# The last multiply-add of a convolution goes from VectorE to ScalarE and GpSimd, and the order of all engines is laid out anew

## The chip, the cores and the metric

One core of a Trainium2 chip runs the whole kernel. The metric is the device time of one execution in microseconds (us), the median of three runs. TensorE (PE) multiplies, VectorE (DVE), ScalarE (ACT) and GpSimd (POOL) do the elementwise work, SyncE (SP) issues the DMAs.

## The reference

```python
scores = q @ k.T / sqrt(64)                       # 8 batches x 8 heads, 576 x 576, q and k 576 x 64
thresh = max(scores, -1) - tau
attn = where(scores >= thresh, exp(scores - max(scores, -1)), 0)
attn = attn / (sum(attn, -1) + 1e-9)
x = concat_heads(attn @ v)                        # 8 x 576 x 512
pre = sum(conv_w[i] * xp[:, i:i+576, :] for i in range(5))   # causal, xp has 4 zero rows in front
out = (sigmoid(pre) * (x @ w_val)) @ w_out        # the weights arrive as float64
```

## The kernel before

**Units of work.** The 64 heads are worked off in 32 pairs (8 batches of 4 pairs). A pair has nine score tiles of 128 rows by 576 keys: one that holds the 64 left-over rows of both heads, and eight of 128 queries of one head; 288 tiles in all. For each tile PE makes the scores `s` in PSUM from split operands (`KH`, `KL`, `Q`; `multiply`, L732, four matmuls), DVE takes the negative row maximum `nm` (`largest`, L736) and the row threshold `th` from it, one number a row (`lowest`, L742), ACT makes `e = exp(s - max)` (`weigh`, L746), and DVE keeps what lies above the threshold, with the row sum (`keep`, L753, into `pp`, `sums`). `keep` sets the score room in PSUM free. There are two such rooms, and a third one until tile `THIRD_UNTIL`, which then becomes the two accumulators `acc` of the products.

**Behind the tiles.** The row sums get their 1e-9 on POOL (L770) and are inverted on DVE (L772); the division of `pp` goes to POOL (L783), ACT (L779) or DVE (L781), whichever is first. PE turns `pp` by matmuls with an identity (`turn`, L836, into `tp`), ACT copies it to `T` (L847), and PE multiplies by `v` (L914, L922). ACT puts the result of a pair into `xT` (L932).

**The convolution** (`convolve`) is done per pair on 128 channels by 576 rows: the first of the five multiply-adds makes `pre` on POOL (`tap0`, L988), the other four run on DVE (`tap`, L993, one instruction each of the form `pre = xT * cw + pre`), and ACT makes the tanh of the gate (L1001). ACT and POOL split `xT` into `xh` and `xl` (L969, L975).

**The products** (`products`, L1052) run once a batch: 96 matmuls for `x @ w_val`, gated by DVE (`val`, L1079), split into `gh` and `gl` (L1100 on ACT, L1107 on POOL), and 96 for the product with `w_out`, taken out by DVE (L1142) or ACT (L1144). The float64 weights are turned into float32 parts by integer steps on DVE, ACT and POOL during the first batch (L321 to L385).

**What sets the order.** The program is laid out by a planner that runs when the kernel is built. Each step is an `op` with an engine, a due time and a planned cost. The due time is the number of the tile plus an offset from a table, `EARLY` for the first 78 tiles and `AT` behind it. `carry_out` takes again and again the step that can begin first, by lowest due time among those, and writes it on its engine. In the plan a DVE step between SBUF operands (`DVEp`) and a POOL step never run at the same time. On the chip each engine then works its list off in that order, and waits by semaphores. Where the plan leaves PE idle in the first part, `keep_busy` (L181) puts in matmuls of the identity whose result nobody reads, one per so many planned us of gap:

```python
if e == "PE" and 1.0 < gap and t < FILL_UNTIL and r_tp.free and r_tp.free[0][0] <= idle["PE"] + 0.2:
    keep_busy(r_tp.free[0][1], int(gap / 0.5))
```

Of the kernel before, what the change touches and what calls it, by code (L numbers as in the profile page):

```python
# [19 lines left out]
DIVIDE = ("DVEp", "ACT")  # L20
PACE_M = 0.124
THIRD_UNTIL = 38
LOWEST = 0
SHARED = (0, 1, 3, 6, 7)
REST = 'DVE'
SPREAD = False
ALONE = 0
AMONG = ("DVEp",)
# [10 lines left out]
AT = dict(
    score=-33.05, largest=-102.51, lowest=-23.11, weigh=-37.49, keep=-24.88, add=23.1, inv=-56.23,  # L40
    divide=59.56, turn=-22.26, copy=19.76, attend=-23.83, evac=-22.31, fetch=96.26, high_k=128.92,
    low_k=67.78, scale_q=4.66, high_q=12.66, low_q=1.99, place=-132.6, copies=-77.08, copies_q=56.7,
    fetch_v=22.69, prep=-27.65, early1=49.11, early2=54.51, early3=29.03, conv_high=20.77,
    tap0=-0.84, conv_low=-16.76, tap=-34.66, tap_step=11.87, gate=-12.05, products=-6.3, val=94.33,
    g_high=43.79, g_low=162.74, out=99.25, send=53.84, words=-4.76, words_step=7.01,
    words_fetch=0.77, split=35.72, words_sub=-25.09, words2=-1.91, cw=-6.65, corner=-6.73,
)

EARLY = dict(
    score=-5.33, largest=-82.82, lowest=163.7, weigh=-36.29, keep=13.11, add=-6.03, inv=-37.4,  # L50
    divide=28.57, turn=0.66, copy=-20.26, attend=2.02, evac=-61.15, fetch=97.48, high_k=23.73,
    low_k=18.92, scale_q=50.26, high_q=46.36, low_q=8.75, place=15.59, copies=54.04,
    copies_q=165.86, fetch_v=25.8, prep=-4.29, early1=15.1, early2=13.7, early3=23.08,
    conv_high=21.07, tap0=-30.63, conv_low=22.96, tap=5.74, tap_step=0.34, gate=-109.04,
    products=14.86, val=-11.89, g_high=20.21, g_low=13.29, out=-36.55, send=-68.92, words=-5.8,
    words_step=8.17, words_fetch=-14.64, split=119.57, words_sub=9.29, words2=-3.84, cw=-128.53,
    corner=-82.08,
)
# [6 lines left out]
def tile_thresholded_attention_gated_mix(  # L65
# [64 lines left out]
    def due_of(k, what, at=None):  # L130
        return k + (EARLY if (k if at is None else at) < EARLY_UNTIL else AT)[what]
# [62 lines left out]
    def carry_out():  # L194
        while True:
# [764 lines left out]
    def convolve(pair, batch, k, js):  # L960
# [29 lines left out]
        def tap(i):  # L990
# [283 lines left out]
```

## Time and profile before

| | |
|---|---|
| median of 3 runs (lowest to highest) | 731.37 us (730.84 to 732.71) |
| the profiled execution: its time, and its span from first to last instruction | 730.5 us, 728.7 us |
| busy share of the span | PE 96%, PE's weight loads (PEld) 84%, DVE 91%, ACT 81%, POOL 64% |
| DMA, share of 16 engines | 53% |

Busy time counts a stretch in which at least one instruction of the engine is under way. Instructions of one engine overlap at their ends, so the sum of their durations is more than the busy time. The time of the execution is 1.8 us more than its span.

### The profile page before, as it was taken

Reading aid. Unit: us, or ns where it says so; the run is one execution under the profiler, and the core shown is the slowest. Engines: PE = TensorE matmul, PEld = TensorE weight load, DVE = VectorE, ACT = ScalarE, POOL = GpSimd, SP = SyncE. Lnnn points to the kernel's source line nnn. Section 1 sums busy time; section 2 is a strip of 40 time slices with the busy share of each in tenths; the row PEclk is TensorE's granted clock in tenths of the full one; section 3 lists DMA queues with packets and bytes.
Section 4 is the critical chain, followed back from the end, with each engine's and each line's share of the span. In section 5 each row is a group of like instructions: output and inputs, shape, how many; then the busy total and the mean of one; then the engine's idle time right before and its main releaser. Section 6 shows DMA issues by size and latency. Waiting matters only on the chain.

```text
span 728.7 us, 16203 instructions
## 1 busy us (share of the span) xinstructions
PE 702.0 (96%) x5272; PEld 609.2 (84%) x5272; DVE 660.2 (91%) x1618; ACT 591.6 (81%) x1167; POOL 467.8 (64%) x690
## 2 busy tenths in 40 slices
PE   7789888999999999999999999999999999999998
PEld 6566656888888998888889898888988888898988
DVE  7999998999999988999999999999999999899842
ACT  6999997898878898877889887887878887898730
POOL 3788677887677747686566765677456865655231
PEclk9999999999999999999999999999999999999999
DMA  6886655537565666356664655556664446540001
GB/s 219 211 203 181 164 137 156 113 87 184 165 147 126 151 178 152 98 137 159 158 152 113 152 149 152 129 125 168 160 160 117 112 137 169 144 98 19 34 33 66
DMA packets 60883, 100.54 MB, mean 138 GB/s; under 512 B 18688, under 2 KB 20096, under 8 KB 60800
## 3 DMA queue, kind: packets, MB, share of 16 engines
q1 hardware_dynamic: 60512, 98.96, 53.1%
q8 instruction: 42, 0.69, 0.4%
q10 hardware_dynamic: 288, 0.56, 0.2%
q14 instruction: 41, 0.34, 0.1%
HBM read 35.18 MB, written 9.44 MB: 61 GB/s over the span
## 4 chain that ended last, share of the span: by engine, by line
PE 83%; DVE 7%; ACT 5%; DMA 2%; issue 1%; POOL 1%; SPq 0%; ACTq 0%; POOLq 0%; DVEq 0%
PE acc L1052 26%; PE s L732 19%; PE tp L836 17%; PE acc L922 9%; PE tp L922 6%; DVE pp L753 2%; PE acc L914 2%; DVE nm L736 2%; ACT e L746 2%; PE tp L914 2%; ACT T L847 1%; ACT pp L779 1%; DMA pre<-w_out 1%; DVE pre L993 1%; PE tp L181 1%
## 5 line engine op out<-in xcount | busy, mean ns | idle before, releaser
L736 DVE TENSOR_REDUCE nm<-s 128x1 f32<-128x576 f32 x276 | 204.8, 753 | 22.0 <-PE s L732 18.2
L746 ACT ACTIVATE e<-s,nm 128x576 f32<-128x576 f32 x276 | 204.2, 753 | 13.9 <-DVE nm L736 11.8
L753 DVE SCALAR_TENSOR_TENSOR pp<-s,th,e 128x576 f32<-128x576 f32 x244 | 196.8, 812 | 9.6 <-ACT e L746 5.6
L847 ACT COPY T<-tp 128x384 f32<-128x384 f32 x384 | 175.0, 493 | 18.3 <-PE tp L836 17.0
L836 PE MATMUL tp<-ident,pp 128*128 128x128 f32 x1152 | 176.9, 274 | 8.6 <-ACT T L847 4.6
L732 PE MATMUL s<-KH,Q 128*128 128x288 f32 x488 | 147.7, 320 | 8.4 <-DVE pp L753 3.5
L836 PEld LDWEIGHTS tp<-ident,pp 128*128 128x128 f32 x1152 | 137.2, 140 | 16.9 <-ACT T L847 6.8
L732 PE MATMUL s<-KL,Q 128*128 128x288 f32 x488 | 135.9, 295 | 0.0
L783 POOL TENSOR_SCALAR pp<-pp,sums 128x576 f32<-128x576 f32 x132 | 105.9, 807 | 25.6 <-DVE sums L772 10.7
L993 DVE SCALAR_TENSOR_TENSOR pre<-xT,cw,pre 128x576 f32<-128x576 f32 x128 | 120.5, 943 | 0.7
L732 PEld LDWEIGHTS s<-KH,Q 128*128 128x128 f32 x488 | 92.0, 188 | 23.1 <-issue 9.8
L779 ACT ACTIVATE pp<-pp,sums 128x576 f32<-128x576 f32 x102 | 79.3, 790 | 23.1 <-DVE sums L772 22.6
L770 POOL TENSOR_SCALAR sums<-sums 128x2 f32<-128x2 f32 (+1 forms) x160 | 44.6, 279 | 76.6 <-DVE pp L753 63.3
L732 PEld LDWEIGHTS s<-KL,Q 128*128 128x128 f32 x488 | 92.1, 189 | 0.0
L1052 PE MATMUL acc<-xh,wvh 128*128 128x256 f32 (+1 forms) x256 | 78.5, 307 | 1.6 <-ACT xT L891 1.3
L1052 PE MATMUL acc<-gh,woh 128*128 128x256 f32 (+1 forms) x256 | 78.8, 308 | 0.0
L1052 PE MATMUL acc<-gh,wol 128*128 128x256 f32 (+1 forms) x256 | 78.5, 307 | 0.0
L1052 PE MATMUL acc<-xh,wvl 128*128 128x256 f32 (+1 forms) x256 | 78.4, 306 | 0.0
L1052 PE MATMUL acc<-gl,woh 128*128 128x256 f32 (+1 forms) x256 | 78.1, 305 | 0.0
L1052 PE MATMUL acc<-xl,wvh 128*128 128x256 f32 (+1 forms) x256 | 77.8, 304 | 0.0
L461 POOL TENSOR_TENSOR ql<-q_r,qh 128x320 fp32r<-128x320 f32 (+1 forms) x62 | 59.1, 969 | 23.3 <-ACT qh L455 20.0
L447 POOL TENSOR_TENSOR kl<-k_r,kh 128x320 fp32r<-128x320 f32 x62 | 57.2, 929 | 22.7 <-ACT kh L441 12.9
(116 smaller groups left out, 1386.9 us busy)
## 6 DMA issues: line engine op xcount, KB each, us to landing
KH<-kh SPq DMA_DIRECT2D x124, 144.0 KB, 2.6
KL<-kl SPq DMA_DIRECT2D x124, 144.0 KB, 3.2
v<-vs SPq DMA_DIRECT2D x32, 320.0 KB, 3.1
k_r<-kT SPq DMA_DIRECT2D x31, 320.0 KB, 3.9
q_r<-qT SPq DMA_DIRECT2D x31, 288.0 KB, 3.2
outT<-o SPq DMA_DIRECT2D x28, 288.0 KB, 2.1
Q<-qh SPq DMA_DIRECT2D x62, 128.0 KB, 2.7
Q<-ql SPq DMA_DIRECT2D x62, 128.0 KB, 3.6
```

Of the source, the lines that this page charges most:

```text
L461: engine.tensor_sub(self.ql[:, x:y], self.q_r[:, x:y], self.qh[:, x:y].bitcast(F32))
L732: nc.tensor.matmul(s[:, a, :HS], w, m, start=i == 0, stop=i == len(terms) - 1)
L736: nc.vector.tensor_reduce(self.nm, self.s[:, :, :HS], axis=AX.XY, op=ALU.max, negate=True)
L746: nc.scalar.activation(self.e, self.s[:, :, :HS], AF.Exp, bias=self.nm)
L753: nc.vector.scalar_tensor_tensor(grp.p[:, i * S : (i + 1) * S].rearrange("p (a f) -> p a f", a=2), self.s[:, :, :HS], self.th, self.e, op0 ...
L779: nc.scalar.mul(v, v, ri(i))
L783: nc.gpsimd.tensor_scalar(v, v, ri(i), 0.0, op0=ALU.mult, op1=ALU.add)
L836: nc.tensor.transpose(tp[:, i * P : (i + 1) * P], self.p[:, k0 : k0 + P], ident)
L847: engine(T[:, c0 : c0 + n, self.off : self.off + P], tp[:, 0 : n * P].rearrange("p (c q) -> p c q", q=P),)
L922: nc.tensor.matmul(a[hs, : W[half.j]], t.v[:, c0 : c0 + D], half.T[:, h * NKC + c, 0 : W[half.j]], start=False, stop=c == NKC - 1, skip_gr ...
L993: nc.vector.scalar_tensor_tensor(cv, pair.xT[:, i + a : i + z], cw[:, g, i : i + 1], cv, op0=ALU.mult, op1=ALU.add)
L1052: nc.tensor.matmul(taken[name, e, j][:, :w], wt[:, c, c0 : c0 + P], moving(c, i)[:, hs], start=n == 0, stop=n == NM - 1,)
```

## The change

- The last of the four multiply-adds on DVE (`i = 4`) becomes two steps: ACT multiplies `xT` by the weight into a new room `tmp` (L1007 of the changed kernel), and POOL adds `tmp` to `pre` (L1013). There is one `tmp`; `ql` has one room instead of two.
- The row threshold (L742) may go to POOL for any tile (`LOWEST` 0 to 300), where the planner finds POOL free earlier.
- The unread matmuls in PE's gaps are counted by `(gap - 0.6) / 0.115` instead of `gap / 0.5`.
- All due offsets are others, the third score room stays until tile 42 instead of 38, the products are spaced by 0.421 instead of 0.124 of a tile, and two planned costs are larger (one DMA issue 0.62 instead of 0.58, a POOL step with two inputs by 0.04).

```diff
-PACE_M = 0.124
-THIRD_UNTIL = 38
-LOWEST = 0
+PACE_M = 0.421
+THIRD_UNTIL = 42
+LOWEST = 300
...
+APART = (4,)
...
-    score=-33.05, largest=-102.51, lowest=-23.11, weigh=-37.49, keep=-24.88, add=23.1, inv=-56.23,
+    score=-80.76, largest=-174.57, lowest=-22.68, weigh=-66.2, keep=-108.45, add=93.41, inv=-170.32,
...
-                keep_busy(r_tp.free[0][1], int(gap / 0.5))
+                keep_busy(r_tp.free[0][1], int((gap - 0.6) / 0.115))
...
+        def scaled(i):
+            def run():
+                room["tmp"] = r_tmp.take()
+                nc.scalar.mul(room["tmp"], pair.xT[:, i + a : i + z], cw[:, g, i : i + 1])
+
+            return run
+
+        def added():
+            cv = batch.pre[:, g, a:z]
+            nc.gpsimd.tensor_add(cv, cv, room["tmp"])
...
         for i in range(1, KT):
-            last = op("DVEp", due_of(k, "tap") + due_of(0, "tap_step", k) * i, tapped(n), tapped(n) + 0.11, tap(i), [last])
+            due = due_of(k, "tap") + due_of(0, "tap_step", k) * i
+            if i in APART:
+                times = op("ACT", due, act(n), act(n) + 0.18, scaled(i), [pair.got_x, conv_ready], [r_tmp])
+                last = op("POOL", due, pool2(n), pool2(n) + 0.1, added, [last, times], gives=[(r_tmp, lambda: room["tmp"])])
+            else:
+                last = op("DVEp", due, tapped(n), tapped(n) + 0.11, tap(i), [last])
```

What stands on the engines then, counted over the whole program: DVE has 96 multiply-adds instead of 128, 198 thresholds instead of 288, 41 copies of the result instead of 34, and one division more. ACT has 32 multiplications and 4 divisions more and 7 copies of the result fewer. POOL has 32 additions and 90 thresholds more and 5 divisions fewer. PE has 48 unread matmuls instead of 26, and else the same. Of the 90 thresholds on POOL 8 belong to the first 54 tiles.

**PE at the start of the program.** The first rows of PE's list, up to the scores of the second tile (`tp` is the room that the unread matmuls write, `s` the scores). Before:

```order
L181 MATMUL tp_101<-ident 128x128 x14
L732 MATMUL s_103<-KH_119,Q_117 128x288
L732 MATMUL s_103<-KL_121,Q_117 128x288
L732 MATMUL s_103<-KH_119,Q_117 128x288
L732 MATMUL s_103<-KL_121,Q_117 128x288
L181 MATMUL tp_101<-ident 128x128 x3
L732 MATMUL s_104<-KH_119,Q_117 128x288
```

The changed kernel at the same place:

```order
L183 MATMUL tp_101<-ident 128x128 x20
L735 MATMUL s_103<-KH_118,Q_116 128x288
L735 MATMUL s_103<-KL_120,Q_116 128x288
L735 MATMUL s_103<-KH_118,Q_116 128x288
L735 MATMUL s_103<-KL_120,Q_116 128x288
L183 MATMUL tp_101<-ident 128x128 x8
L735 MATMUL s_104<-KH_118,Q_116 128x288
```

Fourteen unread matmuls ahead of the first scores became twenty, three ahead of the second scores became eight, and the next block, behind the scores of the third tile, has thirteen instead of seven.

**DVE at the start of the program**, from the maxima of the second and third tile on (`cw`, `whole` and `o` belong to the float64 steps of the weights). Before:

```order
L736 TENSOR_REDUCE nm_128<-s_104 128x1
L736 TENSOR_REDUCE nm_129<-third 128x1
L323 TENSOR_SCALAR cw_179<-cw_raw 128x20
L323 TENSOR_SCALAR o_173<-pre_161 128x512
L325 SCALAR_TENSOR_TENSOR cw_178<-cw_raw,cw_179 128x20
L742 TENSOR_SCALAR th_131<-nm_127,less 128x1
L327 SCALAR_TENSOR_TENSOR cw_178<-cw_180,cw_178 128x20
L325 SCALAR_TENSOR_TENSOR whole_175<-pre_161,o_173 128x512
L329 TENSOR_SCALAR cw_179<-cw_178 128x20
L753 SCALAR_TENSOR_TENSOR pp_137,sums_139<-s_103,th_131,e_125 128x576
L742 TENSOR_SCALAR th_132<-nm_128,less 128x1
```

The changed kernel there:

```order
L739 TENSOR_REDUCE nm_127<-s_104 128x1
L739 TENSOR_REDUCE nm_128<-third 128x1
L756 SCALAR_TENSOR_TENSOR pp_136,sums_138<-s_103,th_130,e_124 128x576
L745 TENSOR_SCALAR th_132<-nm_128,less 128x1
L756 SCALAR_TENSOR_TENSOR pp_136,sums_138<-s_104,th_131,e_125 128x576
L739 TENSOR_REDUCE nm_129<-s_103 128x1
L756 SCALAR_TENSOR_TENSOR pp_134,sums_139<-third,th_132,e_124 128x576
L775 RECIPROCAL sums_138<-sums_138 128x2
L745 TENSOR_SCALAR th_133<-nm_129,less 128x1
```

The six steps of the weights that stood ahead of the first `keep` stand behind the first tiles now, and two of the first thresholds are gone to POOL.

**POOL in the middle of the program**, around the steps of the pair whose low half goes to `xl_157`. Before:

```order
L310 TENSOR_SCALAR pl_138<-pl_138 128x64
L461 TENSOR_TENSOR ql_113<-q_r_107,qh_112 128x320
L461 TENSOR_TENSOR ql_113<-q_r_107,qh_112 128x256
L770 TENSOR_SCALAR sums_140<-sums_140 128x2
L988 TENSOR_SCALAR pre_161<-xT_147,cw_178 128x576
L975 TENSOR_TENSOR xl_157<-xT_147,xh_151 128x320
L783 TENSOR_SCALAR pp_135<-pp_135,sums_140 128x576
L975 TENSOR_TENSOR xl_157<-xT_147,xh_151 128x256
L770 TENSOR_SCALAR sums_141<-sums_141 128x2
L469 TENSOR_SCALAR q_r_107<-q_r_107,sc 128x576
L783 TENSOR_SCALAR pp_137<-pp_137,sums_141 128x576 x2
L770 TENSOR_SCALAR sums_142<-sums_142 128x2
```

The changed kernel there:

```order
L773 TENSOR_SCALAR sums_139<-sums_139 128x2
L464 TENSOR_TENSOR ql_113<-q_r_107,qh_112 128x320
L464 TENSOR_TENSOR ql_113<-q_r_107,qh_112 128x256
L1013 TENSOR_TENSOR pre_160<-pre_160,tmp_162 128x576
L991 TENSOR_SCALAR pre_160<-xT_147,cw_178 128x576
L978 TENSOR_TENSOR xl_157<-xT_147,xh_151 128x320
L978 TENSOR_TENSOR xl_157<-xT_147,xh_151 128x256
L773 TENSOR_SCALAR sums_140<-sums_140 128x2
L472 TENSOR_SCALAR q_r_107<-q_r_107,sc 128x576
L745 TENSOR_SCALAR th_132<-nm_128,less 128x1
L786 TENSOR_SCALAR pp_135<-pp_135,sums_140 128x576 x2
L773 TENSOR_SCALAR sums_141<-sums_141 128x2
```

The addition (L1013) of the pair before stands directly ahead of the first multiplication (L991) of this pair, and a threshold (L745) stands between the row sums and the division.

## Rows read from the trace of the kernel before

**Rows 1.** Busy time of each engine in five stretches (x: instructions); PEld are the weight loads, PEclk the granted clock of TensorE as a share of full speed.

```profile
20.00:135.00 115.00, 99.42 (x680) 74.33 (x678) 109.54 (x274) 106.64 (x208) 87.44 (x119) 1.00 0.69 173
135.00:300.00 165.00, 163.17 (x1247) 142.69 (x1245) 153.36 (x369) 138.56 (x278) 118.26 (x170) 1.00 0.57 142
300.00:400.00 100.00, 100.00 (x773) 89.28 (x774) 96.08 (x243) 84.78 (x166) 65.63 (x103) 1.00 0.56 141
400.00:697.00 297.00, 296.10 (x2279) 260.72 (x2275) 275.55 (x675) 243.62 (x483) 180.82 (x269) 1.00 0.49 125
697.00:728.70 31.70, 28.70 (x216) 28.49 (x215) 11.03 (x21) 5.46 (x12) 8.75 (x11) 0.99 0.13 47
```

The columns are: the stretch, its length, then PE, PEld, DVE, ACT, POOL, PEclk, the DMA share and GB/s.

**Rows 2.** Who waited for whom from 20 to 135 us, the rows of PE's weight loads: us in total, times, longest us.

```profile
PEld tp L836 <- ACT T L847: 7.6, 11, 1.8
PEld s L732 <- DVE pp L753: 5.9, 12, 1.5
PEld tp L836 <- POOL pp L783: 2.2, 3, 1.0
PEld acc L1052 <- ACT xT L891: 1.5, 1, 1.5
PEld tp L836 <- ACT pp L779: 1.3, 3, 0.6
```

**Rows 3.** Who waited for whom from 135 to 697 us: PE's rows, and one of DVE.

```profile
PEld s L732 <- DVE pp L753: 3.7, 5, 1.3
PEld s L732 <- DVE pre L993: 2.7, 7, 0.4
PEld tp L836 <- POOL pp L783: 0.6, 2, 0.4
PEld tp L836 <- ACT xT L932: 0.4, 1, 0.4
...
DVE nm L736 <- PE s L732: 16.7, 43, 1.5
```

**Rows 4.** Groups of instructions over the whole span: line, engine, operation, out and in, count, busy us, mean ns of one, and the idle time ahead of them.

```profile
L993 DVE SCALAR_TENSOR_TENSOR pre<-xT,cw,pre 128x576 f32<-128x576 f32 x128 | 120.5, 943 | 0.7
L742 DVE TENSOR_SCALAR th<-nm,less 128x1 f32<-128x1 f32 x288 | 54.8, 207 | 0.7
L779 ACT ACTIVATE pp<-pp,sums 128x576 f32<-128x576 f32 x102 | 79.3, 790 | 23.1 <-DVE sums L772 22.6
L781 DVE TENSOR_SCALAR pp<-pp,sums 128x576 f32<-128x576 f32 x22 | 11.4, 524 | 0.2
L1142 DVE TENSOR_SCALAR o<-acc 128x320 f32<-128x320 f32 (+1 forms) x34 | 15.6, 458 | 15.6 <-PE acc L1052 15.2 <-DMA bdq<-ql 0.3
```

**Rows 5.** The same view for 20 to 120 us alone.

```profile
L993 DVE SCALAR_TENSOR_TENSOR pre<-xT,cw,pre 128x576 f32<-128x576 f32 x11 | 10.2, 927 | 0.0
L742 DVE TENSOR_SCALAR th<-nm,less 128x1 f32<-128x1 f32 x46 | 8.2, 204 | 0.0
L779 ACT ACTIVATE pp<-pp,sums 128x576 f32<-128x576 f32 x22 | 17.1, 807 | 0.0
L783 POOL TENSOR_SCALAR pp<-pp,sums 128x576 f32<-128x576 f32 x16 | 12.6, 795 | 3.2 <-DVE th L742 1.5 <-PE s L732 1.0 <-DVE sums L772 0.4
L770 POOL TENSOR_SCALAR sums<-sums 128x2 f32<-128x2 f32 (+1 forms) x25 | 7.4, 295 | 4.8 <-DVE pp L753 2.9 <-DVE pl L753 0.3
L339 POOL TENSOR_TENSOR whole<-whole,wvh 128x512 f32<-128x512 f32 x4 | 5.6, 1402 | 2.0 <-DVE wvh L336 1.9
```

**Rows 6.** Instructions in order of time at the start, PE's first and then DVE's: start us, duration us, engine, line, operation, count, and in brackets the idle time before and its releaser. An unread matmul counts as two here.

```profile
1.36 4.75 PE L181 MATMUL tp<-ident 128*128 128x128 f32 x28 [1.36 <-POOL ident masks.py:199]
5.87 0.38 PE L732 MATMUL s<-KH,Q 128*128 128x288 f32 x1
...
9.52 1.73 PE L181 MATMUL tp<-ident 128*128 128x128 f32 x14
13.94 0.37 PE L732 MATMUL s<-KH,Q 128*128 128x288 f32 x1 [2.69 <-DVE th L742]
...
5.46 1.13 DVE L588 TENSOR_TENSOR KL<-pp,KH 128x288 fp32r<-128x288 f32 x2
6.69 0.76 DVE L736 TENSOR_REDUCE nm<-s 128x1 f32<-128x576 f32 x1
...
12.98 0.81 DVE L753 SCALAR_TENSOR_TENSOR pp<-s,th,e 128x576 f32<-128x576 f32 x1
...
17.60 0.76 DVE L736 TENSOR_REDUCE nm<-s 128x1 f32<-128x576 f32 x1 [1.10 <-PE s L719]
```

**Rows 7.** Busy time as in the first group, for 14 to 18 us.

```profile
14.00:18.00 4.00, 3.88 (x17) 3.57 (x18) 2.90 (x9) 3.19 (x5) 2.92 (x5) 0.57 0.14 30
```

**Rows 8.** DVE and POOL in order of time around 94 us.

```profile
94.28 1.88 DVE L993 SCALAR_TENSOR_TENSOR pre<-xT,cw,pre 128x576 f32<-128x576 f32 x1
...
94.28 1.27 POOL L385 TENSOR_TENSOR wol<-whole,woh 128x512 fp32r<-128x512 f32 x1
95.53 1.24 POOL L783 TENSOR_SCALAR pp<-pp,sums 128x576 f32<-128x576 f32 x1
```

**Rows 9.** ACT and DVE in order of time in the last 30 us.

```profile
703.26 0.69 ACT L1001 ACTIVATE pre<-pre 128x576 f32<-128x576 f32 x1 [0.27 <-DVE pre L993]
...
707.36 0.49 DVE L1079 SCALAR_TENSOR_TENSOR g<-pre,acc 128x320 f32<-128x320 f32 x1 [1.27 <-PE acc L1052]
```

More of the change, by code (lines that the diff above doesn't have):

```diff
@@ L34 @@
 ROOMS = dict(
-    kr=1, qr=1, kh=2, kl=2, qh=1, ql=2, v=2, Q=2, KH=2, KL=2, bd=2, e=2, pp=3, pl=1, T=(2, 1), xT=2,
-    xh=6, xl=6, g=2, gh=4, gl=4, o=2,
+    kr=1, qr=1, kh=2, kl=2, qh=1, ql=1, v=2, Q=2, KH=2, KL=2, bd=2, e=2, pp=3, pl=1, T=(2, 1), xT=2,
+    xh=6, xl=6, tmp=1, g=2, gh=4, gl=4, o=2,
 )
 AT = dict(
-    score=-33.05, largest=-102.51, lowest=-23.11, weigh=-37.49, keep=-24.88, add=23.1, inv=-56.23,
-    divide=59.56, turn=-22.26, copy=19.76, attend=-23.83, evac=-22.31, fetch=96.26, high_k=128.92,
@@ L42 @@
[L42 to L46, printed above, removed]
+    score=-80.76, largest=-174.57, lowest=-22.68, weigh=-66.2, keep=-108.45, add=93.41, inv=-170.32,
@@ new lines @@
+    divide=100.48, turn=-0.84, copy=-27.37, attend=-6.95, evac=8.14, fetch=179.5, high_k=210.73,
+    low_k=140.59, scale_q=75.77, high_q=44.8, low_q=-2.53, place=-33.72, copies=-105.43,
+    copies_q=59.1, fetch_v=23.37, prep=-27.65, early1=91.1, early2=12.43, early3=8.95,
+    conv_high=0.54, tap0=-22.97, conv_low=89.88, tap=-41.41, tap_step=16.87, gate=-38.79,
+    products=40.51, val=11.89, g_high=-31.35, g_low=128.18, out=183.36, send=6.8, words=-4.76,
+    words_step=7.01, words_fetch=0.77, split=35.72, words_sub=-25.09, words2=-1.91, cw=-6.65,
@@ L47 @@
+    corner=-6.73,
 )
 EARLY = dict(
[L50 to L55, printed above, removed]
@@ L56 @@
-    words_step=8.17, words_fetch=-14.64, split=119.57, words_sub=9.29, words2=-3.84, cw=-128.53,
-    corner=-82.08,
+    score=-0.94, largest=-147.46, lowest=156.58, weigh=-46.73, keep=117.46, add=2.28, inv=-100.97,
+    divide=32.43, turn=4.96, copy=-23.65, attend=-28.38, evac=-7.19, fetch=151.45, high_k=-31.61,
+    low_k=17.09, scale_q=92.29, high_q=-6.94, low_q=15.14, place=-87.83, copies=17.55,
+    copies_q=167.95, fetch_v=-4.77, prep=-4.29, early1=15.1, early2=13.7, early3=23.08,
+    conv_high=-0.42, tap0=-23.52, conv_low=28.59, tap=13.94, tap_step=0.41, gate=-32.24,
@@ L58 @@
+    products=12.11, val=73.26, g_high=36.28, g_low=8.68, out=-49.91, send=-6.91, words=-8.43,
+    words_step=10.73, words_fetch=88.79, split=50.64, words_sub=-34.7, words2=-11.37, cw=-88.26,
+    corner=-85.66,
 )
@@ L285, in tile_thresholded_attention_gated_mix @@
     r_pre = Rooms(mix, 2, [P, NE, S], F32, "pre")
+    r_tmp = Rooms(mix, ROOMS["tmp"], [P, S], F32, "tmp")
     r_g = Rooms(mix, ROOMS["g"], [P, S], F32, "g")
@@ L289, in tile_thresholded_attention_gated_mix @@
     r_o = Rooms(mix, ROOMS["o"], [P, S], F32, "o")
-    SEND = 0.58
+    SEND = 0.62
     def act(n):
@@ L303, in pool2 @@
     def pool2(n):
-        return 0.17 + 0.00212 * n
+        return 0.21 + 0.00212 * n
     def tapped(n):
@@ L997, in tap @@
             return run
+        room = {}
+        def scaled(i):
[6 more added lines that the diff above has]
+            nc.gpsimd.tensor_add(cv, cv, room["tmp"])
         def gate():
```

## The prediction

> **What bounds the kernel now.** I read the busy times stage by stage first [rows 1]. From 300 to 400 us PE is busy all the time, and its weight loads fill 89.28 of 100 us. I take that as PE's full rate, since the weight loads don't hide a wait inside a matmul's end. Measured by it, 20 to 135 us loses 115 - 74.33 / 0.8928 = 31.7 us, 135 to 300 us loses 165 - 142.69 / 0.8928 = 5.2 us, and 400 to 697 us loses 297 - 260.72 / 0.8928 = 5.0 us. The last 31.7 us hold 216 products, one behind the other, 28.70 / 216 = 0.133 us each. So there are two kernels here. Up to 135 us the elementwise engines set the pace: DVE is busy for 109.5 and ACT for 106.6 of 115 us, since the weights are made there and no products fill the gaps. Behind that PE sets the pace and nothing else can gain more than 10.2 us.
>
> The waits tell who is late. In the first stage PE's weight loads wait mostly for ACT (7.6 + 1.5 + 1.3 = 10.4 us), then for DVE's `keep` (5.9), then for POOL (2.2) [rows 2]. In the second stage nearly all is DVE: 3.7 us for `keep` and 2.7 us for the multiply-adds, together 6.4, against 0.6 for POOL and 0.4 for ACT; and DVE itself waits 16.7 us for PE there [rows 3].
>
> **The change, part by part.** Whole-program loads first. DVE loses 32 multiply-adds of 0.943 us and 90 thresholds of 0.207, and gets 7 copies of 0.458 and a division of 0.524: -30.2 - 18.6 + 3.2 + 0.5 = -45 us [rows 4]. ACT's new multiplication has the form of its division (SBUF to SBUF, 576 columns, a factor per row), 0.790 us: 32 + 4 of these less 7 copies of about 0.4 are +26 us. POOL's addition of 576 columns isn't in the trace. Its nearest row is the addition of 512 columns, 1.402 us [rows 5]; by columns that is 1.58 us, which I take, between 0.795, a one-input step of that width [rows 5], and 1.88, a multiply-add that POOL held up [rows 8]. With 90 thresholds at the price of another tiny POOL step, 0.295 [rows 5], and 5 divisions less, POOL gets 50.6 + 26.6 - 4 = +73 us.
>
> *First stage (B).* Counted in the lists up to the 54th tile, which the trace reaches at about 135 us, DVE has 4 multiply-adds and 8 thresholds fewer and 2 divisions more: -4 x 0.927 - 8 x 0.204 + 2 x 0.524 = -4.3 us [rows 4, 5]. ACT has 4 multiplications more: +4 x 0.807 = +3.2. POOL has 3 additions and 8 thresholds more and 3 divisions less: 4.7 + 2.4 - 2.4 = +4.7. What PE gets depends on who is late. By the waits that is ACT for 10.4 and DVE for 5.9 us; weighted so, (10.4 x 3.2 - 5.9 x 4.3) / 16.3 = +0.5. I take 0, since a new order may shift work between the two. The bounds are -4.3 (DVE alone decides) and +3.2 (ACT alone).
>
> *Start (C).* An unread matmul counts as two in the trace, and 14 of these take 1.73 us, 0.12 each [rows 6]. So the six more ahead of the first scores cost 12 x 0.12 = 1.4 us: the scores begin at 7.3 instead of 5.87, and DVE, whose last split ends at 6.59, begins its first maximum 1.3 us later. The formula counts 0.115 us for what takes 0.24, so every block outlasts its gap. The third block then starts 1.3 us later than at 9.52, and its thirteen take 3.1 us, to about 13.9, while the first `keep`, with some 2 us of weight steps out of its way, could begin about 1 us before 12.98 in spite of the late start, and free the room at 12.9. The fourth scores thus begin where they began before, 13.94, and DVE waits some 0.4 us. Against that stands the clock: from 14 to 18 us it was granted at 0.57, mostly the level of 1.2 GHz, after PE had stood idle for 2.69 us [rows 6, 7], and DVE waited 1.10 us for the slowed scores. With the gap filled that should go. Sum: +1.3 + 0.4 - 1.1 = +0.6, bounds 0 and +2.
>
> *Products behind (D).* When the 54th tile's scores are issued, PE has issued 34 products instead of 43, and 222 transposes instead of 219. PE is the bound from there on, so what is left over is paid: 6 x 0.133 = +0.8. At the end it is even: behind the last scores stand 8 products more and 9 transposes fewer.
>
> *Second stage (E).* Between 135 and 697 us DVE is busy for 525 of 562 us, 93%. There the change takes 28 x 0.943 + 82 x 0.207 - 3.2 = 40 us from it, leaving 86%. ACT (467 busy) gets about 22 and comes to 87%, POOL (365) about 68 and comes to 77%. DVE's 6.4 us of PE's waits should shrink to a small rest; I take -5. The far bound is -10.2, the whole loss. What comes late next is the threshold on POOL: a `keep` now may wait for a POOL step that stands behind an addition. An addition of 1.58 us in a pair's 17.5 us is in the way of one threshold in eleven, and the exponential (0.75 us) covers half, so 82 x 0.09 x 0.6 = 4 us of DVE, which has 14% to spare: nothing on PE, with a bound of +4.
>
> *Hidden.* In the last pair the chain now ends in a POOL addition that stands behind two splits. The gate ran at 703.26, and the step that needs it began at 707.36 [rows 9]: 3.4 us of cover, of which the later addition uses about 3. Cost nothing, +0.8 without cover. `ql` with one room costs nothing: it is handed back by the same step as `qh`, which had one already.
>
> Sum: 0 + 0.6 + 0.8 - 5 = -3.6 us. The profiled execution took 728.7 us of span and 1.8 around it, 730.5, which is 0.9 below the median of the runs. So 730.5 - 3.6 + 0.9 = **727.8 us**.
>
> **A rule against it.** At 94.28 us a multiply-add and a POOL step start together; POOL's takes its usual 1.27, the multiply-add 1.88 instead of some 0.8, and the next POOL step starts at 95.53 and takes 1.24 [rows 8]. So they shut each other out. The Trainium skill, "Perfetto Trace Analysis", section "Optimizing Scalar/DVE Operations", says that VectorE and GpSimd share a read port of SBUF, so that moving work between these two might not help. The trace agrees in this place. What it would make here, from rows: each moved step holds the shared way for 1.58 instead of 0.82 us, so the first stage gets +4.7 - 3.7 = +1.0, and in the second only the thresholds relieve DVE, 17 of 40 us, -2: 0.6 + 0.8 + 1.0 - 2 = +0.4, **731.8 us**. I don't take it as the likeliest, since `keep` and the maximum, which read PSUM, take the same 0.81 and 0.75 us whatever POOL does, and DVE's waits for PE in the second stage leave room.
>
> **The rivals.** *The shared way decides*: 731.8 us, as above, chance 0.12.
>
> *ACT alone sets the first stage*: B is +3.2, and the gain behind it is used up: 0.6 + 0.8 + 3.2 - 5 = -0.4, **731.0 us**, chance 0.12. For it speak ACT's 10.4 us of waits, against it that DVE is as full.
>
> *POOL's list blocks PE*: the addition waits for DVE's third multiply-add, and behind it in POOL's list stand the row sums, the division and so the transposes, at which PE stands in its own list. At 0.3 us of PE per pair for 29 pairs it is +8.7 - 3.6 = +5.1, **736.5 us**. It decides from (3.6 + 2.2) / 29 = 0.2 us per pair on. For it: POOL goes from 65% to 77% with steps twice as long; against: POOL cost PE only 0.6 us there so far. Chance 0.21.
>
> *DVE was the bound everywhere*: B -4.3 and E -6.4 give 0.6 + 0.8 - 10.7 = -9.3, **722.1 us**, chance 0.13.
>
> The forecast itself keeps 0.42, for 723 to 729.
>
> **How the numbers follow.** A measurement of this kernel can tell about 0.3%, 2.2 us, from no change, so faster means below 729.2 and slower above 733.6. Faster has 0.42 + 0.13 = 0.55, no change 0.12 + 0.12 = 0.24, slower 0.21. The range goes from 720, just beyond the largest gain, to 736, where the blocking POOL is half inside; beyond it I leave 0.06 below and 0.1 above.
>
> **What would show it.** Right: DVE busy near 615 us, ACT near 617, POOL near 540; PE's waits for `keep` and the multiply-adds between 135 and 697 us below 2 us; the clock at full from 14 to 18 us; the first scores near 7.3 us; the new addition between 1.4 and 1.7 us; the products' final run 0.8 us shorter, with 210 of them behind the last attention. Wrong: if the 54th tile comes before 131 or behind 138 us, B is wrong; if PE's waits for POOL rise above 5 us, the list of POOL blocks; if DVE's remaining multiply-adds get longer than 1.05 us in the mean, the shared way decides.

## The result, and the profile after

The changed kernel takes 736.8 us in the median of 7 runs (733.5 to 739.5), the kernel before 731.9 beside it (7 runs): ratio 1.0074, 95% interval 1.0054 to 1.0094. By the ratio it is 5.4 us slower (by the two medians 4.9), and the forecast of 727.8 us missed it by 9.0. The profiled execution took 735.27 us with a span of 733.5, so it lies 1.5 us below the median.

The first view is that of [rows 1], for the changed kernel: a stretch, its length, busy time of PE, PEld, DVE, ACT and POOL, the granted clock, the DMA share and GB/s.

```profile
20.00:135.00 115.00, 98.28 (x660) 72.37 (x661) 104.99 (x266) 107.60 (x210) 85.47 (x121) 0.99 0.69 169
135.00:300.00 165.00, 163.42 (x1241) 143.55 (x1241) 146.58 (x347) 147.59 (x293) 129.95 (x192) 1.00 0.55 142
300.00:400.00 100.00, 100.00 (x776) 88.64 (x773) 89.29 (x214) 84.52 (x166) 77.82 (x120) 1.00 0.58 145
400.00:697.00 297.00, 296.65 (x2280) 262.10 (x2278) 266.40 (x625) 252.14 (x492) 215.52 (x343) 1.00 0.48 125
697.00:730.00 33.00, 32.64 (x245) 30.25 (x243) 11.29 (x22) 6.88 (x14) 11.49 (x13) 1.00 0.14 48
```

DVE has become emptier, ACT and POOL fuller, as meant. But PE was busy for 99 to 100% behind 135 us before, and still is. The waits from 135 to 697 us, to be held against [rows 3] (us in total, times, longest us):

```profile
DVE nm L739 <- PE s L735: 42.0, 62, 3.7
...
PEld acc L925 <- issue: 8.6, 26, 0.3
...
PEld s L735 <- issue: 6.2, 16, 0.4
...
PEld s L735 <- DVE pre L996: 1.9, 5, 0.4
...
PE tp L839 <- ACT T L850: 1.6, 3, 0.9
```

DVE now stands 42.0 us waiting for scores, where it stood 16.7: the time that it was given became idle time. And here are rows of the kernel before for the same stretch that the prediction does not use: PE's own waits (not those of its weight loads), and two rows of the loads in which nobody is waited for (`issue`):

```profile
PE s L732 <- DVE pp L753: 2.2, 3, 1.1
PE tp L836 <- ACT xT L932: 0.2, 1, 0.2
...
PEld acc L922 <- issue: 9.0, 27, 0.3
PEld s L732 <- issue: 6.5, 17, 0.4
```

So before the change PE itself waited 2.4 us from 135 to 697 us, for all engines together. After it PE's own wait for `keep` is gone, and one for ACT's copies (`tp`, 1.6 us) stands in its place.

Where the time went can be counted from the trace, in which each matmul has a start. Each kind has its own interval to the next start where nothing is waited for: 0.133 us for a piece of scores, 0.108 for a transpose, 0.148 or 0.118 for a product of 320 or 256 columns, and so on. All matmuls of the kernel times these intervals are 668.1 us, unread ones left out; a stretch less its share of that is what PE lost there. The level depends on the intervals that are taken: with the median of each kind the sum is about 671 us, and the third row has 6.8 and 8.6 instead of 10.6 and 12.1. The changes come out within 0.3 us of those here.

| PE's loss, us | before | after | change | predicted |
|---|---|---|---|---|
| 0 to 20 | 14.5 | 14.5 | 0.0 | +0.6 (C) |
| 20 to 160 | 32.4 | 34.5 | +2.1 | 0 (B) and +0.8 (D) |
| 160 to 700 | 10.6 | 12.1 | +1.5 | -5 (E) |
| behind 700 | 3.1 | 4.3 | +1.2 | 0 |
| sum, the span less 668.1 | 60.6 | 65.4 | +4.8 | -3.6 |

### The profile page after: what moved, and what is told of

Same layout as the page of the kernel before. It is cut to its first block, busy times and chain, and to the rows that moved or that the text cites. A ratio compares the mean times of both kernels' runs of the same rounds, so it can differ in the third digit from the quotient of the medians.

```text
span 733.5 us, 16314 instructions
## 1 busy us (share of the span) xinstructions
PE 708.7 (97%) x5316; PEld 613.8 (84%) x5316; DVE 631.9 (86%) x1504; ACT 611.6 (83%) x1196; POOL 528.4 (72%) x807
## 4 chain that ended last, share of the span: by engine, by line
PE 84%; DVE 6%; ACT 4%; DMA 3%; POOL 2%; issue 1%; SPq 0%; DVEq 0%; ACTq 0%; POOLq 0%
PE acc L1073 26%; PE s L735 19%; PE tp L839 17%; PE acc L925 8%; PE tp L925 6%; PE acc L917 2%; DVE nm L739 2%; DVE pp L756 2%; PE tp L917 2%; PE tp L183 2%; ACT e L749 1%; PE tp L886 1%; ACT T L850 1%; DMA KH<-kh 1%; DMA k_r<-kT 1%
## 5 line engine op out<-in xcount | busy, mean ns | idle before, releaser
L839 PE MATMUL tp<-ident,pp 128*128 128x128 f32 x1152 | 179.7, 275 | 11.7 <-ACT T L850 8.4
L850 ACT COPY T<-tp 128x384 f32<-128x384 f32 x384 | 178.1, 500 | 10.3 <-PE tp L839 9.9
L786 POOL TENSOR_SCALAR pp<-pp,sums 128x576 f32<-128x576 f32 x131 | 101.2, 777 | 17.7 <-DVE sums L775 5.5
L782 ACT ACTIVATE pp<-pp,sums 128x576 f32<-128x576 f32 x103 | 79.5, 789 | 17.7 <-DVE sums L775 17.5
L996 DVE SCALAR_TENSOR_TENSOR pre<-xT,cw,pre 128x576 f32<-128x576 f32 x96 | 90.3, 942 | 0.7
L773 POOL TENSOR_SCALAR sums<-sums 128x2 f32<-128x2 f32 (+1 forms) x160 | 41.8, 261 | 50.4 <-DVE pp L756 35.7
L464 POOL TENSOR_TENSOR ql<-q_r,qh 128x320 fp32r<-128x320 f32 (+1 forms) x62 | 61.5, 1003 | 10.1 <-ACT qh L458 8.4
L925 PE MATMUL acc<-T,v 128*64 128x320 f32 x432 | 64.1, 439 | 0.0
```

What stands on the lines that cost most here:

```text
L464: engine.tensor_sub(self.ql[:, x:y], self.q_r[:, x:y], self.qh[:, x:y].bitcast(F32))
L782: nc.scalar.mul(v, v, ri(i))
L786: nc.gpsimd.tensor_scalar(v, v, ri(i), 0.0, op0=ALU.mult, op1=ALU.add)
L839: nc.tensor.transpose(tp[:, i * P : (i + 1) * P], self.p[:, k0 : k0 + P], ident)
L850: engine(T[:, c0 : c0 + n, self.off : self.off + P], tp[:, 0 : n * P].rearrange("p (c q) -> p c q", q=P),)
L925: nc.tensor.matmul(a[hs, : W[half.j]], t.v[:, c0 : c0 + D], half.T[:, h * NKC + c, 0 : W[half.j]], start=False, stop=c == NKC - 1, skip_gr ...
```

## The experiments

Two theories stood at first. "Order": the new order of the lists loses time, and PE had nothing to win. "Parts": the work put on POOL and ACT costs PE. "Start" was a third one for the unread matmuls. An order is kept by writing the exchanged instruction where the other one stood, without planning anew.

### The parts exchanged, each order kept

The new order with the old parts:

```diff
-                keep_busy(r_tp.free[0][1], int((gap - 0.6) / 0.115))
+                keep_busy(r_tp.free[0][1], int(gap / 0.5))
...
-                   other=[("POOL", 0.26, 0.36, lambda: self.lowest(nc.gpsimd))] if k < LOWEST else []),
+                   other=[("POOL", 0.26, 0.36, lambda: self.lowest(nc.vector))] if k < LOWEST else []),
...
-                nc.scalar.mul(room["tmp"], pair.xT[:, i + a : i + z], cw[:, g, i : i + 1])
...
-                last = op("POOL", due, pool2(n), pool2(n) + 0.1, added, [last, times], gives=[(r_tmp, lambda: room["tmp"])])
+                last = op("POOL", due, pool2(n), pool2(n) + 0.1, tap(i), [last, times], gives=[(r_tmp, lambda: room["tmp"])])
```

> The changed kernel's order of all engines, with the three exchanged parts put back at the same places of that order: the fifth multiply-add is one DVE instruction again (at the place of the POOL addition), the 90 thresholds are on DVE again, and the unread matmuls are counted by gap / 0.5. What is left of the change is the order alone. Kernel before 731.9, changed kernel 736.8 us. Theory 'order': the loss is in the new order (first stage 20 to 120 us, where steps that PE waits for come late), and PE had nothing to win behind it: 735 to 738 us. Theory 'parts' (POOL's 32 additions and 90 thresholds cost PE time): 731 to 733 us. Theory 'start' (more unread matmuls delay the first scores): 734.5 to 735.5, the same as the changed kernel with the old count alone. DVE gets 40 us of work back, and if relieving it was worth the 5 us that I forecast, this kernel must be slower than the changed one, about 741.

Measured: 745.6 us, ratio 1.0190 (1.0169 to 1.0211), beyond every range above; only the sign of the last sentence came true. PE's loss from 160 to 700 us is 21.8 us instead of the changed kernel's 12.1. Its waits from 135 to 697 us say for whom:

```profile
PEld s L735 <- DVE pp L756: 8.7, 15, 1.1
...
PE s L735 <- DVE pp L756: 5.4, 8, 0.9
```

The old order with the new parts (`ON_POOL` are the 90 tiles; the new count of unread matmuls is in it too, and `ql` with one room):

```diff
+            if self.k in ON_POOL:
+                engine = nc.gpsimd
...
+                if i == 2:
+                    nc.scalar.mul(tmp, pair.xT[:, 4 + a : 4 + z], cw[:, g, 4:5])
+                if i == 4:
+                    nc.gpsimd.tensor_add(cv, cv, tmp)
+                    return
```

> The kernel before in its own order, with the three exchanged parts alone: the fifth multiply-add as an ACT multiplication (at the place of the third one) and a POOL addition (at its own place), the thresholds of the same 90 tiles on POOL at their place, and the new count of unread matmuls. Theory 'order': the parts neither give nor take, since PE waited for DVE only 2.2 us itself behind 135 us: 731 to 733 us, with DVE's busy time 45 us lower. Theory 'parts': the loss comes with them, 735 to 738. My forecast's step on the second stage (PE's 6.4 us of weight-load waits for DVE can be won) would make it 726 to 729. Theory 'start': 733 to 734, and all of the loss is there in the run with the new count alone.

Measured: 738.6 us, 1.0090 (1.0070 to 1.0110), 0.6 above the range of "parts". DVE's waits from 135 to 697 us in this run:

```profile
DVE nm L744 <- PE s L740: 32.5, 69, 1.6
DVE pp L763 <- ACT e L756: 10.2, 25, 1.1
DVE pp L763 <- POOL th L752: 8.3, 17, 1.5
```

In the old order `keep` (`pp`) waits 8.3 us for thresholds on POOL and 10.2 for exponentials. The same rows of the changed kernel have 3.7 us for the exponential and none for a threshold:

```profile
DVE pp L756 <- ACT e L749: 3.7, 15, 0.6
```

So the new order fits the parts in better. Each order is bad with the other's parts, and both of my theories fell in their simple form: this exchange can't separate order and parts.

### One part at a time

In the new order the fifth multiply-add alone goes back to DVE, by the last two pieces of the first diff above:

> The changed kernel in its own order with the fifth multiply-add alone put back: one DVE instruction at the place of the POOL addition, no ACT multiplication. With both moved parts put back (and the old count of unread matmuls) this order gave 745.6 us, 8.9 more than the changed kernel. DVE gets 32 x 0.943 = 30 us of work back, of 49 us that both parts take from it. Theory 'DVE's load': the cost goes by DVE's busy time, 740.5 to 743.5. Theory 'thresholds': the threshold on DVE sits right ahead of the keep that frees the score room, so the thresholds hold most of the 9 us: 736.5 to 739. Theory 'multiply-adds': 743 to 746.

Measured: 743.2 us, 1.0141 (1.0117 to 1.0165): at the upper end of "DVE's load" and at the lower end of "multiply-adds", so it doesn't tell these two apart; "thresholds" is out. In the old order the 90 thresholds alone go to POOL, by the first piece of the second diff:

> The kernel before in its own order, with the thresholds of the same 90 tiles as in the changed kernel moved to POOL at the place that they have on DVE; the multiply-adds stay. All three parts together cost 7 us in this order (738.6 against 731.5), the new count of unread matmuls nothing of it. Theory 'thresholds': a keep waits for a threshold that stands behind another POOL step, and frees the score room late: 735 to 738 us. Theory 'additions': 731 to 733 us.

Measured: 734.0 us, 1.0039 (1.0021 to 1.0058), +2.9 us, between the two ranges. And the multiply-add alone goes to ACT and POOL, by the other piece (with one room for `ql`):

> The kernel before in its own order, with the fifth multiply-add alone moved: ACT multiplies at the place of the third one, POOL adds at the place of the fifth; thresholds and unread matmuls as before. Theory 'additions': steps of POOL that PE waits for (row sums, division) stand behind an addition that waits for DVE, as my third rival had it at 0.2 to 0.3 us per pair: 735 to 738 us. Theory 'thresholds': 731 to 733 us.

Measured: 735.7 us, 1.0054 (1.0039 to 1.0069), +4.0 us. The time lies in the range of "additions", but since the thresholds cost too, neither theory holds alone; the two add up to about the 6.6 us of all three parts. Two waits of this run from 135 to 697 us:

```profile
DVE pp L754 <- ACT e L747: 11.7, 33, 0.7
...
PEld tp L837 <- POOL pp L784: 0.4, 2, 0.3
```

POOL's list does not block PE's transposes, as "additions" had it: PE's weight loads wait for POOL's division 0.4 us. What is late is ACT's exponential: `keep` waits for it 11.7 us, before it was 4.4.

### The work left out

This separates the new order from the moved work. What the change takes from DVE is done by nobody, first in the old order:

```diff
             self.th = r_th.take()
+            self.bar = self.th
+            if self.k in ON_POOL:
+                self.bar = self.nm
+                return
...
+                if i == 4:
+                    return
```

> The kernel before in its own order, with the work that the change takes from DVE left out altogether: no fifth multiply-add (32 of 128), and no threshold of the 90 tiles that the changed kernel gives to POOL (their keep compares with the negated maximum instead). Nothing is put on ACT or POOL for it. So this is the most that relieving DVE of 49 us can bring in the old order. My forecast's step on the second stage says at least -5 us, up to -10: 722 to 727 us. Theory 'PE at its floor': behind 160 us PE loses only some 3 us to waits, so the gain is 0 to 3 us there and at most 4 in the first stage: 728 to 732 us.

Measured: 729.5 us, 0.9970 (0.9952 to 0.9988): -2.2 us, between 0.9 and 3.5, as "PE at its floor" has it. Its page and its waits from 135 to 697 us:

```profile
PE 704.8 (97%) x5272; PEld 612.4 (84%) x5272; DVE 626.0 (86%) x1496; ACT 593.2 (81%) x1167; POOL 463.2 (64%) x690
```

```profile
DVE nm L743 <- PE s L739: 38.8, 76, 1.7
...
PE s L739 <- DVE pp L764: 1.1, 1, 1.1
```

DVE is down to 86%, and its wait for scores is up from 16.7 to 38.8 us, with nothing on ACT or POOL to blame. A free gift of this work brings about what PE's own waits before had said, 2.4 us. By the starts of the matmuls (median intervals) PE loses 2.0 us less from 135 to 697 us in this profile; the profiled execution is not shorter than before (span 729.0 us), since it lost 1.3 us more from 20 to 160 us.

The same in the new order:

```diff
+            if engine is nc.gpsimd:
+                self.bar = self.nm
+                return
...
-                nc.scalar.mul(room["tmp"], pair.xT[:, i + a : i + z], cw[:, g, i : i + 1])
...
-            nc.gpsimd.tensor_add(cv, cv, room["tmp"])
+            return
```

> The changed kernel in its own order, with the same work left out: no ACT multiplication and no POOL addition of the fifth tap, and no threshold on POOL (90 tiles; their keep compares with the negated maximum). Work and DVE load are the same as in the run on the kernel before with this work left out; only the order differs. Theory 'order': the new order's own loss stays, 734 to 737 us, 3 to 6 above the other. Theory 'parts': POOL's additions and thresholds were what cost, and without them it comes to the time of the other run, within 2 us.

Measured: 735.1 us, 1.0054 (1.0036 to 1.0072), as "order" has it. With the same work, the new order is 6.1 us behind the old one by the ratios (1.0054 - 0.9970 of 731.7), give or take 1.9. The two profiles differ by 3.9 us; by the starts of the matmuls PE loses 3.4 us more in the new order from 160 to 700 us, 1.3 more from 20 to 160 and 0.6 less ahead of that. "Order" here takes in what the planner placed with it: 7 copies of the result and a division on DVE that ACT and POOL did before (DVE is busy for 631.3 us here, 626.0 in the other run), the one room of `ql`, for which no wait shows, and the 22 unread matmuls, which cost nothing that could be told (below).

What the parts cost in their own order, the changed kernel against this run, is 1.0074 - 1.0054, or 1.5 us, give or take 2: not told from nothing. So along this way the 5.4 us are -2.2 for DVE's relief, +6.1 for the order and +1.5 for the parts. The split depends on the way: in the new order the same relief is worth 10 us (745.6 against 735.1), and in the old order the same parts cost 9 (738.6 against 729.5).

### The unread matmuls

The changed kernel's order with the old count (the first piece of the first diff):

> The changed kernel with the old count of unread matmuls, gap / 0.5; all else in the same order. Theory 'start': the first scores begin at about 6 us instead of 8.2, and 1.5 to 2.5 us come back: 734.5 to 735.3 us. Theory 'order': the start is caught up again before tile 9, where the two traces show the same time; and without the unread matmuls the clock falls between 14 and 18 us: 736 to 738.

Measured: 736.7 us, 1.0071 (1.0046 to 1.0096): the same as the changed kernel. Its scores begin at 6.66 instead of 7.97 us, and by the 18th tile that lead is down to 0.6 us (45.6 against 46.2). "Start" is wrong.

The old order with the new count, and with one by what an unread matmul takes in the trace:

```diff
-                keep_busy(r_tp.free[0][1], int(gap / 0.5))
+                keep_busy(r_tp.free[0][1], int((gap - 0.6) / 0.115))
```

> The kernel before with the new count of unread matmuls, (gap - 0.6) / 0.115, and nothing else changed. Theory 'start': first scores at 8.2 instead of 5.87 us, +1 to +2.5 us: 733 to 734.5 us. Theory 'order': the delay is caught up by the full clock from 14 to 18 us, 731.5 to 732.5. My forecast's term for the start was +0.6 us.

Measured: 731.1 us, 0.9991 (0.9977 to 1.0004). With the other count:

```diff
-                keep_busy(r_tp.free[0][1], int(gap / 0.5))
+                keep_busy(r_tp.free[0][1], int((gap - 0.6) / 0.23))
```

> The kernel before in its own order with the unread matmuls counted by (gap - 0.6) / 0.23, which is what one takes by the trace (0.24 us): blocks of 15, 4, 12 and 3 instead of 14, 3, 7 and 2. The new count of the change (20, 8, 25 and 6 in this order) gave 731.1 against 731.5, with fewer stretches at half the clock. Expected if the filled gaps save the slow stretch at 14 to 18 us (1.1 us of DVE's wait) without delaying the first scores: 730 to 731.2 us; if a later slow stretch takes its place: 731 to 732.

Measured: 732.8 us, 1.0011 (0.9995 to 1.0026), above both ranges, but the kernel before also took 732.3 us beside it. No kernel that does all the work could be told faster than the kernel before; the new count in the old order comes nearest to it.

### Laid out anew

In these runs the planner makes the lists again. First the changed kernel with all old offsets:

```diff
-PACE_M = 0.421
-THIRD_UNTIL = 42
+PACE_M = 0.124
+THIRD_UNTIL = 38
...
-    score=-80.76, largest=-174.57, lowest=-22.68, weigh=-66.2, keep=-108.45, add=93.41, inv=-170.32,
+    score=-33.05, largest=-102.51, lowest=-23.11, weigh=-37.49, keep=-24.88, add=23.1, inv=-56.23,
```

> The changed kernel with the offsets, the products' spacing (0.124) and the third room's end (38) of the kernel before, so that the planner lays out the parts (addition on POOL, thresholds where POOL is free, new count of unread matmuls) by the old offsets. In before's order as it stood the three parts cost 7 us (738.6). Theory 'parts': the parts cost PE time in any order that isn't fitted to them, and a planner that knows of them mends some of it: 734 to 738 us. Theory 'offsets': the old offsets were good and the parts are free once they are planned for: 729 to 732. My forecast's steps on the parts alone: 726 to 729.

Measured: 762.0 us, 1.0405 (1.0387 to 1.0424), far beyond every range.

Then the new offsets without the parts:

```diff
-LOWEST = 300
+LOWEST = 0
...
-APART = (4,)
+APART = ()
```

> The changed kernel without the two moved parts: the fifth multiply-add stays on DVE, all thresholds stay on DVE, and the planner lays them out by the new offsets (ql keeps its one room, tmp is not used; new count of unread matmuls). In the changed kernel's order as it stood, putting the parts back cost 9 us (745.6 against 736.8). Theory 'offsets': the new offsets are the worse ones whatever the parts do, and replanning mends only some of the 9 us: 737 to 745. Theory 'parts': without the parts it goes back towards before, 731 to 735.

Measured: 747.7 us, 1.0211 (1.0191 to 1.0231), above "offsets" and far from "parts".

Then the changed kernel with the table `EARLY` alone from before:

```diff
-    score=-0.94, largest=-147.46, lowest=156.58, weigh=-46.73, keep=117.46, add=2.28, inv=-100.97,
+    score=-5.33, largest=-82.82, lowest=163.7, weigh=-36.29, keep=13.11, add=-6.03, inv=-37.4,
```

> The changed kernel with the offsets of the first 78 tiles (EARLY) of the kernel before, planned anew; everything else as in the changed kernel. The changed kernel loses 4.9 us of PE more than before between 20 and 120 us and gets 2.8 back to 160. Theory 'first stage': the new EARLY offsets hold the loss, and this kernel comes to 732 to 734.5 us, with tile 45 kept before 111 us (before 108.5, changed 113.8). Theory 'second stage or parts': the loss comes back elsewhere, 736 to 739.

Measured: 745.9 us, 1.0184 (1.0167 to 1.0201), beyond both ranges. Each table is bad for what it was not made for, and swapping half of one doesn't mend the first stage (the 45th tile's `keep` comes at 119.6 us, against 113.8 in the changed kernel). To see how much of that is the new plan itself, the kernel before was planned anew with a number or two changed that change no work. First the planned costs:

```diff
-    SEND = 0.58
+    SEND = 0.62
...
-        return 0.17 + 0.00212 * n
+        return 0.21 + 0.00212 * n
```

> The kernel before with the two larger planned costs of the change alone (one DMA issue 0.62 instead of 0.58, a POOL step with two inputs 0.04 more), offsets and all else unchanged, laid out anew by the planner. Nothing that an engine does changes, only the order. Theory 'any new layout costs': offsets fit one plan, and laying out anew from them costs several us: 735 to 745 us. Theory 'bad offsets': an order from good offsets stays good, 730 to 734.

Measured: 746.6 us, 1.0199 (1.0178 to 1.0220).

Then the spacing of the products:

```diff
-PACE_M = 0.124
+PACE_M = 0.421
```

> The kernel before with the products' spacing of the change alone (0.421 instead of 0.124 of a tile), laid out anew. Up to the 45th tile the order of PE is the same as before, behind it 5 to 10 products are moved at a time. Theory 'the spacing is the loss': 734 to 738 us, behind 135 us. Theory 'any new layout costs': 734 to 745. Theory 'bad offsets': 730 to 733.

Measured: 743.1 us, 1.0140 (1.0113 to 1.0167).

And the end of the third room:

```diff
-THIRD_UNTIL = 38
+THIRD_UNTIL = 42
```

> The kernel before with the third score room kept until tile 42 instead of 38, laid out anew, all else unchanged. Theory 'the third room': the first products begin later and the first stage loses the 4 us between 27 and 45 tiles that the changed kernel loses: 734 to 737. Theory 'any new layout costs': 734 to 745. Theory 'bad offsets': 730 to 733.

Measured: 737.2 us, 1.0065 (1.0045 to 1.0086). "Any new layout costs" has the direction right three times, and its range twice (the first is 1.6 us above it): 5 to 14 us for lists that do the same work. It is not the order alone, though: the planner also put 4 to 14 divisions on other engines than before, and up to 7 copies of the result from ACT to DVE. The loss moves about with it. From 160 to 700 us PE loses 21.5, 17.7 and 15.6 us in these three against 10.6 before. The new spacing and the third room's end may each be part of the changed kernel's loss; these runs can't say, since a plan with the offsets of another hides it.

## Why the prediction was wrong

**The step that failed is E, the second stage: -5 us were forecast, and +1.5 came.** Of the 8.4 us between the forecast and the two profiles (-3.6 against +4.8) 6.5 lie here. I took PE's loss behind 135 us from the weight loads' share (10.2 us) and DVE's part in it from the weight loads' waits (6.4 us). The size of the loss was about right, 7 to 11 us from 160 us on by starts, but most of it can't be won: some of it is constant, as the idle time of weight loads ahead of the product with `v`, in which nobody is waited for (0.33 us, 27 times before and 26 times after). And a weight load that waits doesn't mean a matmul that waits. The 2.7 us behind the multiply-adds and the 3.7 behind `keep` left 2.2 us on PE itself. The Trainium skill, "TensorE: Matmul & The Clock Gate", section "Architectural detail: the array is 16× 32×32, not 1× 128×128", says that PE may pull weight loads ahead of matmuls that are still under way; the trace agrees, since seven waits of 0.4 us before a weight load (`pre`, [rows 3]) appear in no row of PE. The sign that I had named for this step came as good as true, and still no time came back: PE's weight loads waited 1.9 us for the multiply-adds and 0.2 for `keep`, after 6.4 before, where I had said below 2. With the work left out altogether the gain was 2.2 us. With E at -2.2 my sum would have been 730.6 us, no change.

**What no term stood for is the order itself.** I summed loads, and set 0 for the new order with bounds of -4.3 and +3.2 in the first stage only. With equal work it costs 6.1 us, and plans made anew without any change of work cost 5 to 14. So the quality of the lists is a quantity of its own here, and the sum of loads and waits of the kernel before did not hold it. Where the new order loses is seen in the two profiles (2.1 us up to 160 and 1.5 from there to 700; the 1.2 at the end are not its doing, see the tail below); which of the new offsets is to blame stays open, and PE's own waits (1.8 us from 135 to 697 us, 2.4 before) don't show it.

**B and D together held within B's bounds.** The 54th tile's `keep` came at 135.5 instead of 133.9 us, inside the 131 to 138 named. In between the kernel is later, by 4.2 us at the 31st tile and by 5.3 at the 45th. PE's waits for ACT's copies grew, as these rows of 20 to 135 us show beside [rows 2], where PE's own row (`PE tp`) had 5.4 us in 8 waits:

```profile
PEld tp L839 <- ACT T L850: 10.5, 15, 1.4
PE tp L839 <- ACT T L850: 7.3, 11, 1.2
...
PEld s L735 <- DVE pp L756: 3.8, 9, 1.3
...
PEld s L735 <- DVE pl L756: 1.8, 2, 1.3
...
PEld acc L1073 <- DVE pp L756: 1.6, 1, 1.6
...
PEld third L735 <- DVE pp L756: 1.3, 3, 0.5
```

Waits for ACT's copies rose from 7.6 to 10.5 us. The row of [rows 2] for `keep` fell from 5.9 to 3.8, but with the other three rows here `keep` stands at 8.5 us, after 6.4 before (0.5 of them for `third`). So both are late, and it is not the balance of ACT against DVE that I had set to zero. ACT's new work is not the reason either. The new order with the work left out, where ACT has no new multiplication, has nearly the same waits for the copies:

```profile
PEld tp L843 <- ACT T L854: 10.0, 14, 1.4
...
PE tp L843 <- ACT T L854: 7.1, 12, 1.2
```

**C was right in its sum (0.0 against +0.6, bounds 0 and +2), not in its terms.** The first scores began at 7.97 us, not 7.3: 12 more records of unread matmuls took 2.1 us (0.175 each), not 1.4, since those of the first microseconds are slower than those at 9.52, as [rows 6] had already: 28 records in 4.75 us, 0.17 each. From 14 to 18 us the clock was granted in full, as forecast. But half the clock, the level of 1.2 GHz, came later, behind two idle stretches of PE (ahead of 102.81 and 104.70 us; idle time in brackets):

```profile
102.81 0.55 PE L839 MATMUL tp<-ident,pp 128*128 128x128 f32 x3 [0.98 <-ACT T L850]
...
104.70 0.56 PE L1073 MATMUL acc<-xh,wvh 128*128 128x320 f32 x1 [1.35 <-DVE pp L756]
```

```profile
14.00:18.00 4.00, 3.56 (x28) 3.12 (x27) 3.32 (x9) 3.52 (x6) 3.09 (x6) 1.00 0.46 141
104.80:108.20 3.40, 3.40 (x13) 1.86 (x15) 3.40 (x7) 3.40 (x7) 0.35 (x1) 0.50 0.02 5
```

**The prices were right, the sum of DVE's load was not.** These are groups of the whole span, to be held against [rows 4, 5]:

```profile
L996 DVE SCALAR_TENSOR_TENSOR pre<-xT,cw,pre 128x576 f32<-128x576 f32 x96 | 90.3, 942 | 0.7
L1013 POOL TENSOR_TENSOR pre<-pre,tmp 128x576 f32<-128x576 f32 x32 | 46.3, 1448 | 19.3 <-DVE pre L996 15.9 <-DVE sums L775 3.0
L745 DVE TENSOR_SCALAR th<-nm,less 128x1 f32<-128x1 f32 x198 | 38.8, 209 | 1.6
L745 POOL TENSOR_SCALAR th<-nm,less 128x1 f32<-128x1 f32 x90 | 28.2, 314 | 31.0 <-DVE nm L739 25.5 <-DVE sums L775 4.2 <-DVE th L745 0.2
L1007 ACT ACTIVATE tmp<-xT,cw 128x576 f32<-128x576 f32 x32 | 25.5, 796 | 0.0
```

The addition took 1.45 us (1.58 taken), the multiplication 0.796 (0.790), the threshold on POOL 0.314 (0.295). DVE's busy time fell by 28 us, from 660.2 to 631.9, not by 45. In the run on the old order leaving out 48.8 us of durations took only 34.2 us of busy time, 14.6 / 122 = 0.12 us less for each instruction. Most of that is overlap: in the trace of the kernel before, neighbours on DVE overlap by 0.08 us in the median, 10 of the 14.6 us; the rest stays open. The Trainium skill, "Perfetto Trace Analysis", section "Optimizing Scalar/DVE Operations", says that the acknowledgement of writes, which the profiled latency of an instruction includes, overlaps the next one; the trace agrees in kind.

**The tail.** POOL's addition cost PE nothing there, as forecast, but the last piece of the result found its room `o` not yet written out:

```profile
728.25 0.42 DVE L1163 TENSOR_SCALAR o<-acc 128x256 f32<-128x256 f32 x1 [1.00 <-PE acc L1073]
730.51 0.42 DVE L1163 TENSOR_SCALAR o<-acc 128x256 f32<-128x256 f32 x1 [1.83 <-DMA outT<-o]
```

It waited 1.83 us, 0.83 more than its forerunner waited for PE. That belongs to this execution and not to the change: the transfer that it waited for took 3.10 us from issue to landing, and in the four other profiles of this order the same transfer took 1.69 or 1.70 us and the last piece waited 1.00 us for PE. Behind the last attention stand 210 products instead of 216, as D had it; from the first of them to the end it is 31.2 us in the run with the work left out, 0.8 less than before, and 31.9 here.

**The rivals.** *POOL's list blocks PE* had the time nearly right (736.5) for a reason that isn't there: PE's weight loads waited for POOL 0.5 us from 135 to 697 us. Where the threshold and the multiplication do hurt, in the old order, they delay `keep` by POOL's thresholds and ACT's exponentials. *ACT alone sets the first stage* is not borne out: the first stage is as slow without ACT's multiplications (113.8 us for the 45th tile's `keep` with them, 114.3 without), and no gain came behind it. *The shared way* didn't decide: the remaining multiply-adds took 942 ns, as before (943), though POOL did 117 steps more. The rule of the Trainium skill that I had weighed against the change ("Perfetto Trace Analysis", the section named above) is borne out in its outcome, that moving such work might not help, but not by its reason. *DVE was the bound everywhere* is refuted by the run with the work left out.

## What to carry to other kernels

Before relieving a full engine, leave its work out altogether and time that: it bounds the gain in the order at hand. For a bound engine count only the waits of its own main instructions; waits of loads that run ahead of them were mostly covered here. And where a plan depends on a table of offsets, as here, a new plan can start several us behind (5 to 14 in three plans of the same work), so the gain of a change that needs one has to be larger than the spread between plans.

## What the runs showed of the hardware

The granted clock differs between executions of one kernel, and the time with it: the changed kernel's two runs with a mean clock of 0.997 took 733.5 and 735.3 us, the five with 0.991 to 0.993 took 736.7 to 739.5. In the new order with the old count of unread matmuls the profile (an execution of 739.8 us, the median is 736.7) shows the level of 1.2 GHz over most of three stretches of the first stage:

```profile
29.50:33.50 4.00, 3.70 (x17) 3.28 (x18) 2.89 (x7) 3.43 (x6) 2.22 (x4) 0.57 0.99 237
77.50:84.50 7.00, 6.47 (x29) 5.15 (x27) 5.13 (x14) 6.24 (x12) 4.15 (x7) 0.51 0.26 68
101.00:115.50 14.50, 11.86 (x48) 8.13 (x49) 8.59 (x19) 10.46 (x19) 6.98 (x9) 0.53 0.23 56
```

The 12 runs of the kernel before with the new count had 0.995 to 1.000, the 12 with the count by 0.23 had 0.991 to 0.998, as the kernel before has (0.988 to 0.998). That the fuller blocks keep the clock up is likely by this, but it gave no time that could be told from none.
